# Zero fills moved from the FFN to the last stages and the end of a decode kernel, and six of eight outer products given to VectorE

## The chip, the cores and the metric

The kernel runs on one core of a Trainium2 chip. The metric is the device time of one execution, in microseconds (us). "Span" is the profiled execution from its first to its last instruction; it is 1.7 to 2.4 us shorter than the time of the same execution.

## The reference, cut to what matters

The kernel computes the output and all gradients of one decode step: conditioning (six vectors sa, ca, ga, sb, cb, gb from `silu(c) @ w_mod`), attention of one query over the last 4,096 of 65,536 cached keys and values, then a gated FFN.

```python
mod = (_silu(c) @ w_mod).reshape(c.shape[0], 6, 1, -1)
h = _layernorm(x) * (1 + ca) + sa
x = x + ga * A(h, k_cache, v_cache, wq, wo)     # attends to the last W = 4096 positions
h = _layernorm(x) * (1 + cb) + sb
x = x + gb * B(h, w_gate, w_up, w_down)         # h = sigmoid(g) * u; h @ w_down
# outputs: x, and the gradients of A_x, k_cache, v_cache, wq, wo, w_gate, w_up, w_down, c, w_mod
```

Positions that the window doesn't reach have gradient zero. So 61,440 of 65,536 rows of both cache gradients, 120 MiB in all, are only zeros that must be written. That is nearly half of the 256 MB which the kernel moves.

## The kernel before

The zeros are written by 120 transfers of 1 MiB ("fills"), issued from GpSimd between the real loads and stores. Lists at the head of the kernel say how many fills stand at each point of the program; `zero` takes the next ones and stops when none is left.

```python
Z_FFN = [3, 0, 3, 1, 4, 0, 3, 1, 4, 0, 3, 0, 3, 0, 4, 2, 3, 2, 3, 1, 3, 6, 0, 3, 1, 7, 3, 1]
...
def zero(n, after=None):
    for _ in range(n):
        if not zleft:
            return
        ins = nc.gpsimd.dma_start(out=zleft.pop(0).bitcast(FP32), in_=zeros[:, :])
        ...
```

The FFN goes through 14 blocks. Each loads 0.5 MiB of w_down and 1 MiB of w_up and w_gate, and turns the loaded tiles in place into their gradients, which it stores. A tile is loaded again when its store has landed. The last store of a block, the gradient of w_gate (`dwg_view`), is called the dWgate store below.

```python
for n in range(NB):
    ...                                            # front: matmuls with h; dug broadcast to all rows
    nc.sync.dma_start(out=wd_dram(out_8, n), in_=wd)
    ...                                            # per 128 rows: a reduction (VectorE), an outer product (ScalarE)
    nc.gpsimd.dma_start(out=dwu_view[:, :, n * FB:(n + 1) * FB], in_=ug[:, 0, :, :])
    st = nc.gpsimd.dma_start(out=dwg_view[:, :, n * FB:(n + 1) * FB], in_=ug[:, 1, :, :])
    if n + 2 < NB:
        dep(load_wd(n + 2), st)                    # the w_down load waits for the dWgate store
    zero(Z_FFN[2 * n])
    if n + 3 < NB:
        load_ug(n + 3)
    zero(Z_FFN[2 * n + 1])
```

The last stores are the sa/ca part of the gradient of w_mod: eight outer products of 128x2048 and eight stores of 512 KB.

```python
for j in range(KD):
    if j % 2 == 0:
        outer_act(s2_t[j], cs_col[:, j:j + 1], dmod_b2)      # ScalarE
    else:
        outer_dve(s2_t[j], cs_col[:, j:j + 1], dmod_b2)      # VectorE
    nc.gpsimd.dma_start(out=dwm_view[:, j, 0:2048], in_=s2_t[j])
    zero(0 if j < KD - 1 else len(zleft))
```

## Time and profile before

| | |
|---|---|
| Time | 632.7 us (632.57 to 632.85, 3 runs) |
| Span of the profiled run | 631.5 us (its time: 633.23) |
| Busy share: TensorE, VectorE, ScalarE, GpSimd | 29%, 51%, 34%, 22% |
| Moved | 70.3 MB read, 185.6 MB written |
| FFN, about 178 to 432 us | 404 GB/s |
| Later stages, 432 to 592 us | 422 to 424 GB/s |
| Tail, 592 to 626 us | 386, then 309 GB/s |

The costliest groups of the page have line, engine, operation, tiles and count; then busy time and the mean ns of one; then the engine's idle time before them and what ended it:

```profile
L139 POOL DMA_DIRECT2D out_dram<-zeros x120 | 65.1, 547 | 209.1 <-DMA out_dram<-zeros 51.3
L174 DVE CUSTOM_DVE_ANT_0 junk<-arena,b1k 128x1024 fp8e4<-128x1024 bf16 x28 | 34.3, 1224 | 111.3 <-DMA arena<-in_B_w_down_dram 110.8
```

The first line is the 120 fills: GpSimd often waits for an earlier transfer before it may issue the next (51.3 us for fills). In the trace its transfers take eight semaphores in turn, so no more than eight are in flight. The second line is the FFN's first work on a w_down tile: VectorE stands idle 110.8 us for those loads. That is not yet a loss. The loads stand in a full queue.

### The profile page before, as it was taken

How to read it: one execution, taken by the hardware profiler on the slowest of the kernel's cores; microseconds unless marked ns; L12 is line 12 of the kernel's file. 1: busy time of each engine (PE TensorE's matmuls, PEld its weight loads, DVE VectorE, ACT ScalarE, POOL GpSimd, SP SyncE). 2: the span in 40 equal slices, each digit the busy share in tenths (PEclk: the TensorE clock that was granted, in tenths of full speed). 3: DMA queues.
4: the chain of work that ended last, by engine and by line, in shares of the span. 5: the costliest groups of instructions: out<-in, count | busy, mean ns of one | idle time of the engine just before them, and what ended most of it. 6: DMA issues, size and time to landing. Idle time of an engine off the chain costs nothing.

```text
span 631.5 us, 8419 instructions
## 1 busy us (share of the span) xinstructions
PE 183.6 (29%) x3324; PEld 161.7 (26%) x3324; DVE 322.9 (51%) x726; ACT 215.4 (34%) x335; POOL 139.5 (22%) x224
## 2 busy tenths in 40 slices
PE   3977275532031110101111101102420950052440
PEld 3977154522021111101111101101310640042330
DVE  3532055204984552535555334507899760699421
ACT  2741165100044231333333023303686340042561
POOL 1001011113315132333332233222221111122021
PEclk9956598655555555555555555555555755555555
DMA  9999999999999999999999999999999999999986
GB/s 358 422 420 421 420 420 418 425 425 426 420 377 404 400 409 406 400 406 391 395 405 419 400 400 407 421 416 427 415 424 425 423 423 427 420 427 423 398 332 246
DMA packets 42183, 256.42 MB, mean 406 GB/s; under 512 B 4768, under 2 KB 4768, under 8 KB 17568
## 3 DMA queue, kind: packets, MB, share of 16 engines
q0 software_dynamic: 31104, 192.95, 80.4%
q1 hardware_dynamic: 10992, 62.93, 28.6%
q8 instruction: 26, 0.43, 0.3%
q14 instruction: 13, 0.11, 0.0%
q10 hardware_dynamic: 48, 0.01, 0.0%
HBM read 70.26 MB, written 185.60 MB: 405 GB/s over the span
## 4 chain that ended last, share of the span: by engine, by line
DMA 64%; DVE 17%; PE 7%; issue 5%; ACT 3%; POOL 2%; ACTq 0%; SPq 0%; DVEq 0%; POOLq 0%
DMA out_dram<-arena 25%; DMA arena<-in_B_w_down_dram 11%; DVE arena L174 7%; DMA arena<-in_A_wq_dram 7%; DMA arena<-in_A_v_cache_dram 6%; DMA arena<-in_B_w_gate_dram 5%; DMA arena<-in_A_wo_dram 4%; ACT arena L205 3%; DMA out_dram<-zeros 3%; DMA arena<-in_w_mod_dram 2%; DVE junk L174 2%; DVE arena L170 2%; DVE arena L178 1%; DVE fold_ps L178 1%; PE tp_kv L404 1%
## 5 line engine op out<-in xcount | busy, mean ns | idle before, releaser
L139 POOL DMA_DIRECT2D out_dram<-zeros x120 | 65.1, 547 | 209.1 <-DMA out_dram<-zeros 51.3
L174 DVE CUSTOM_DVE_ANT_0 junk<-arena,b1k 128x1024 fp8e4<-128x1024 bf16 x28 | 34.3, 1224 | 111.3 <-DMA arena<-in_B_w_down_dram 110.8
L600 PE MATMUL bc_ps<-ident_bf,dug_bf 128*128 128x128 bf16 x56 | 14.5, 475 | 214.4 <-DVE hh L157 214.4
L205 ACT ACTIVATE arena<-dug_b,h 128x512 bf16<-128x512 bf16 x112 | 71.4, 712 | 15.5 <-DVE dh2acc L174 15.5
L174 DVE CUSTOM_DVE_ANT_0 arena<-arena,dug_b 128x512 bf16<-128x512 bf16 x112 | 69.6, 684 | 0.0
L600 PEld LDWEIGHTS <-dug_bf 128*128 128x128 bf16 x56 | 7.8, 171 | 215.5 <-DVE hh L157 215.5
L602 ACT CAST dug_b<-bc_ps 128x512 bf16<-128x512 f32 x14 | 8.2, 586 | 159.4 <-PE bc_ps L600 159.4
L174 DVE CUSTOM_DVE_ANT_0 arena<-arena 128x1024 bf16<-128x1024 bf16 (+1 forms) x16 | 45.1, 2819 | 28.3 <-DMA arena<-in_w_mod_dram 26.2
L784 PEld LDWEIGHTS <-arena 8*128 8x128 bf16 x256 | 25.8, 131 | 76.7 <-issue 73.1
L174 DVE CUSTOM_DVE_ANT_0 arena<-arena,b1k 128x1024 bf16<-128x1024 bf16 x32 | 37.2, 1218 | 0.0
L502 POOL DMA_DIRECT2D arena<-in_B_w_up_dram x14 | 12.7, 909 | 90.3 <-DMA out_dram<-arena 77.7
L205 ACT ACTIVATE arena<-b1k,o_sh 128x1024 bf16<-128x1024 bf16 x24 | 27.2, 1152 | 11.0 <-DVE do_sh L174 11.0
L788 ACT CAST arena<-ps_kv 128x512 bf16<-128x512 f32 x32 | 16.1, 692 | 41.6 <-DMA out_dram<-arena 41.6
L166 DVE COPY arena<-tp_kv 128x1024 bf16<-128x1024 bf16 x19 | 13.0, 691 | 30.2 <-PE tp_kv L404 20.8
L404 PE MATMUL tp_kv<-ident_bf,arena 128*128 128x128 bf16 x256 | 21.2, 246 | 23.7 <-DMA arena<-in_A_k_cache_dram 13.8
L784 PE MATMUL ps_kv<-DO_hd,arena 8*128 8x128 bf16 x128 | 15.9, 296 | 41.6 <-ACT arena L788 41.6
L790 ACT ACTIVATE arena<-ps_kv 128x512 bf16<-128x512 f32 x32 | 16.1, 625 | 29.0 <-DMA out_dram<-arena 29.0
L313 PEld LDWEIGHTS <-arena 128*128 128x128 bf16 x320 | 25.3, 122 | 0.0
L404 PEld LDWEIGHTS <-arena 128*128 128x128 bf16 x256 | 18.4, 112 | 26.5 <-DMA arena<-in_A_k_cache_dram 14.7
L618 POOL DMA_DIRECT2D out_dram<-arena x14 | 12.6, 902 | 56.1 <-ACT arena L205 51.0
L784 PE MATMUL ps_kv<-Q_hd,arena 8*128 8x128 bf16 x128 | 16.1, 295 | 29.1 <-ACT arena L790 29.1
L407 ACT COPY arena<-tp_kv 128x1024 bf16<-128x1024 bf16 x13 | 13.2, 1012 | 33.0 <-PE tp_kv L404 33.0
(224 smaller groups left out, 481.0 us busy)
## 6 DMA issues: line engine op xcount, KB each, us to landing
out_dram<-zeros POOLq DMA_DIRECT2D x120, 1024.0 KB, 17.9
out_dram<-arena POOLq DMA_DIRECT2D x32, 1024.0 KB, 19.5
out_dram<-arena POOLq DMA_DIRECT2D x36, 512.0 KB, 11.5
arena<-in_A_wq_dram SPq DMA_DIRECT2D x16, 1024.0 KB, 15.3
arena<-in_w_mod_dram SPq DMA_DIRECT2D x8, 1536.0 KB, 19.2
arena<-in_A_wo_dram SPq DMA_DIRECT2D x8, 1024.0 KB, 40.7
arena<-in_B_w_down_dram SPq DMA_DIRECT2D x14, 512.0 KB, 10.9
arena<-in_B_w_up_dram POOLq DMA_DIRECT2D x14, 512.0 KB, 11.2
```

Of the source, the lines that this page charges most:

```text
L139: ins = nc.gpsimd.dma_start(out=zleft.pop(0).bitcast(FP32), in_=zeros[:, :])
L166: return nc.vector.tensor_copy(out=out, in_=a)
L174: return nc.vector.tensor_tensor_reduce(out=out, in0=w, in1=b, scale=1.0, scalar=0.0, op0=ALU.mult, op1=ALU.add, accum_out=acc)
L205: return nc.scalar.activation(out=out, in_=b, func=ACT.Copy, scale=col)
L313: nc.tensor.transpose(tp[:, nb * P:(nb + 1) * P], wm_t[j][:, c0:c0 + P], ident_bf[:, :])
L404: nc.tensor.transpose(tp[:, t8 * P:(t8 + 1) * P], src[:, g, t_ * DH:(t_ + 1) * DH], ident_bf[:, :])
L407: last = nc.scalar.copy(out=o, in_=tp[:, :])
L502: nc.gpsimd.dma_start(out=ug_slot[n % 3][:, 0, :, :], in_=wu_view[:, :, n * FB:(n + 1) * FB])
L600: nc.tensor.matmul(ps4[:, k // 2, :, k % 2], lhsT=r["dug_bf"][:, k:k + 1].broadcast_to([P, P]), rhs=ident_bf[:, :], start=(k == 0), stop=( ...
L784: nc.tensor.matmul(ps[:, t4 * DH:(t4 + 1) * DH], lhsT=rows[32 * g:32 * g + HG, t_ * P:(t_ + 1) * P], rhs=hd[32 * g:32 * g + HG, :], start= ...
L788: nc.scalar.copy(out=o, in_=ps[:, :])
L790: nc.scalar.activation(out=o, in_=ps[:, :], func=ACT.Copy, scale=float(scale))
```

## The change

The FFN gets 14 fills less: on average one per block. Four of them run in the last stages instead. Ten fills are held back and placed around the eight last stores, where the DMA share falls. And VectorE makes six of the eight sa/ca tiles, so that ScalarE's slower ones don't hold up the stores.

```diff
-Z_FFN = [3, 0, 3, 1, 4, 0, 3, 1, 4, 0, 3, 0, 3, 0, 4, 2, 3, 2, 3, 1, 3, 6, 0, 3, 1, 7, 3, 1]
+Z_FFN = [3, 0, 2, 1, 3, 0, 2, 1, 3, 0, 2, 0, 3, 0, 3, 1, 2, 2, 2, 1, 2, 4, 0, 3, 1, 5, 3, 1]
+Z_END = [4, 0, 0, 0, 2, 0, 0, 0, 4]
...
+    keep = [sum(Z_END)]
...
-            if not zleft:
+            if len(zleft) <= keep[0]:
                 return
...
+    keep[0] = 0
+    zero(Z_END[0])
     for j in range(KD):
-        if j % 2 == 0:
+        if j % 4 == 1:
             outer_act(s2_t[j], cs_col[:, j:j + 1], dmod_b2)
         else:
             outer_dve(s2_t[j], cs_col[:, j:j + 1], dmod_b2)
         nc.gpsimd.dma_start(out=dwm_view[:, j, 0:2048], in_=s2_t[j])
-        zero(0 if j < KD - 1 else len(zleft))
+        zero(Z_END[1 + j] if j < KD - 1 else len(zleft))
```

## The prediction

> **What bounds the kernel now.** I read the page's slices first, then the windows by stage, then the tail in windows of 1 us, the chain of waits, and at last the landing records of the single transfers in the trace. The slices:
>
> ```profile
> DMA  9999999999999999999999999999999999999986
> HBM read 70.26 MB, written 185.60 MB: 405 GB/s over the span
> ```
>
> The DMA engines have work in every slice but the last two, and no compute engine is above 51% of the span (VectorE). So the kernel is bound by moving 256.4 MB. The windows by stage (start:end, length, then busy time of PE, PEld, DVE, ACT, POOL, then clock, mean DMA share, GB/s) tell where it moves more slowly:
>
> ```profile
> 178.00:432.00 254.00, 32.14 (x712) 30.75 (x712) 122.40 (x377) 75.24 (x147) 76.59 (x110) 0.50 1.14 404
> 432.00:516.00 84.00, 35.97 (x567) 27.92 (x568) 73.15 (x148) 53.84 (x74) 16.22 (x29) 0.54 1.12 422
> 545.00:592.00 47.00, 15.28 (x124) 12.39 (x124) 46.45 (x39) 15.96 (x32) 10.46 (x17) 0.50 1.08 424
> 592.00:612.00 20.00, 11.51 (x142) 9.62 (x139) 1.59 (x11) 11.42 (x22) 3.69 (x7) 0.50 0.95 386
> 612.00:626.00 14.00, 0.37 (x1) 0.08 (x1) 4.11 (x13) 6.48 (x4) 4.72 (x8) 0.50 0.80 309
> ```
>
> The FFN (178 to 432) runs at 404 GB/s, the stages after it at 422 to 424, and the tail from 592 falls to 386 and 309. That fall is what the change aims at. In windows of 1 us:
>
> ```profile
> 611.00:612.00 1.00, 0.38 (x1) 0.08 (x1) 0.50 (x4) 1.00 (x1) 0.00 (x0) 0.50 0.54 221
> 612.00:613.00 1.00, 0.00 (x0) 0.00 (x0) 1.00 (x3) 1.00 (x2) 0.00 (x0) 0.50 0.13 51
> 613.00:614.00 1.00, 0.00 (x0) 0.00 (x0) 1.00 (x2) 1.00 (x1) 0.91 (x1) 0.50 0.06 25
> 614.00:615.00 1.00, 0.00 (x0) 0.00 (x0) 0.00 (x1) 1.00 (x2) 0.66 (x3) 0.50 0.37 152
> ...
> 626.00:627.00 1.00, 0.00 (x0) 0.00 (x0) 0.00 (x0) 0.00 (x0) 0.00 (x0) 0.50 0.07 29
> 627.00:628.00 1.00, 0.00 (x0) 0.00 (x0) 0.00 (x0) 0.00 (x0) 0.00 (x0) 0.50 0.07 29
> ```
>
> This looks like a hole of about 2.9 us (4 minus 0.54, 0.13, 0.06 and 0.37). But look at 613 and at 626 to 628: a share of 0.06 to 0.07, at 25 to 29 GB/s, is one engine of sixteen (1/16 is 0.0625) still at work. The mean hides one engine that is behind. The chain of waits has its mark:
>
> ```profile
> 601.05 14.98 DMA out_dram<-arena
> ...
> 616.06 0.75 DVE arena L170
> ```
>
> The last dWq store is issued at 601.05 and counts as landed only at 616.03, though the mean traffic had run out by 612. The trace records sixteen landings for each transfer, and they explain it. For that store fifteen are in by 609.83 and the sixteenth comes at 616.03; for the last dV/dK store 613.44 and 618.55. The sixteenth landings of the eight sa/ca stores are at 619.83, 621.08, 622.31, 623.57, 624.83, 626.07, 627.30 and 628.53: one per 1.24 us, 2.48 us per MiB, through the hole and to the end. From 545.80 to 628.53 that engine lands 33 MiB in 82.7 us, 2.51 us per MiB, with no gap. It has fallen behind since about 200 us (0.4 us there, 1 at 240, 3 at 400, 6 from 500 on). So the bound is one late DMA engine which never idles in the tail; the hole is in the other fifteen. Its losses are earlier: summing its landings against 2.475 us per MiB (the usual step of a zero fill), it is about 8 us behind at 200, 20 at 400, 25 at 542 and still 24 at the end. 244 MiB by 2.475 is 604 us; the 24 and 3 us after the last landing give the 631.5 us span.
>
> **What the Trainium skill says.** "Perfetto Trace Analysis", section What "DMA-bound" means, lists "Specific DMA engines" as one form of that bound; the trace agrees (one share of 0.06 alone at work). "DMA: Bandwidth & Descriptors", section Why a DMA increments its semaphore by 16 and not by 1: the engines finish independently and only the full sixteen means landed; the landings above show it, 6.2 us apart. The same page, Latency and other measured facts, says that DMA engines 7 and 15 are usually slower in traces; the trace shows one late engine but not its number. "VectorE: DVE Perf Modes", The perf-mode tier table, has 693 ns for a tensor_scalar of 2048 bf16; here 738 ns by the view below.
>
> **The change part by part.** The lists of fills hold more than the 120 regions, and `zero` stops when none is left, so I count what really runs. Before: 36 fills ahead of the FFN, 64 in it, 11 in the dWo stage, 9 in the last stages (the list there would allow 28), none at the end. After: 36, 50, 11, then 13 until ten are left, and 10 at the end (4 ahead of the first sa/ca store, 2 after the fourth, 4 after the last). Nothing is added or removed in bytes.
>
> - FFN: 14 fewer fills by 2.475 us = 34.7 us shorter, if the FFN stays bound by the transfers. Its own extra does not go with them. On the late engine, block periods of 6, 8 and 6 MiB took 16.01 (244.38 to 260.39), 20.55 and 16.65 us, so 1.2, 0.8 and 1.8 us over 2.475 per MiB: it belongs to the gate and up strips, not to the fills.
> - Last stages: 4 more fills, +9.9 us. VectorE is busy 46.5 of 47 us between 545 and 592, but GpSimd waits for free queue places there, so these fills lengthen the queue, not VectorE's work.
> - End: 10 fills, +24.75 us on the late engine. It had no gap, so none of it is hidden.
> - The sa/ca tiles:
>
> ```profile
> L205 ACT ACTIVATE arena<-arena,cs_col 128x2048 bf16<-128x2048 bf16 x4 | 7.7, 1990 | 0.0
> L170 DVE TENSOR_SCALAR arena<-arena,cs_col 128x2048 bf16<-128x2048 bf16 x4 | 2.8, 738 | 2.1 <-DMA out_dram<-arena 2.1
> ```
>
> ScalarE's share goes from 4 by 1.99 = 8 us to 2 tiles, 4 us; VectorE's from 4 to 6 by 0.74 = 4.4 us. The tiles can be ready about 3 us sooner, but four fills (10 us) now stand before them in the queue. Worth nothing on the path.
>
> Sum: -34.7 + 9.9 + 24.75 = 0. Bytes moved along a queue whose slowest engine is always full leave the time as it is: 632.7 us, give or take what the FFN's new pace and the fuller tail do to the engines' skew.
>
> **The rivals.**
> 1. The hole is real time. Then filling 611 to 615 (2.9 us) and the dip at 592 to 596 (share 0.85 of 4 us, 0.6 us) gives about 629. For it: the mean share, and ScalarE running 7.7 us without a pause ahead of the stores. Against it: the sixteenth landings, 1.24 us apart through the hole.
> 2. The FFN starves with fewer fills. Its loop runs through store landing and w_down load:
>
> ```profile
> 260.09 10.88 DMA out_dram<-arena
> ...
> 271.40 13.53 DMA arena<-in_B_w_down_dram
> ```
>
> Two blocks took 36.6 us from store to store (223.51 to 260.09), of which 23.9 are transfer waits (10.94 and 12.96) and about 12.7 compute. At 50 fills a block averages 3 + 3.57 = 6.57 MiB, 16.3 us and its extra 1.2, so 17.5; two are 35.0, and the waits must shrink to 22.3. Blocks of 16 us did run in a row (w_down loads issued at 289.80, 305.74, 321.73), and much of each wait is queueing, which falls as the queue empties. Should the blocks miss the full cut by 0.5 us each, the time is 632.7 + 7 = 640; if no block got shorter, 667, which I exclude.
> 3. The shorter queue after the FFN leaves a gap at the w_mod load that stalls VectorE (527.45 to 542.3, when nothing new is queued). When stores resume at 545.2, the late engine still has transfers to land until 558, 13 us of stock. I estimate the stock at the end of the FFN at some 5 us less (two fills fewer in the last blocks), so no gap; if there is one, +1 to 3 us.
> 4. The ends of the engines draw together in the tail. It helps only if the late engine gets faster when the others keep busy; nothing shows that.
>
> **Range and chances.** The null sum has 632.7. Rival 1, at about one in six, pulls down by up to 3.5 us; rivals 2 and 3, at about one in six, pull up by 2 to 7. I take 632.3, and 629.0 to 636.0 for 8 in 10. Two per cent is 12.7 us: more than the whole tail loss of rival 1, and reachable upwards only if the FFN clearly starves. So faster 0.02, same 0.95, slower 0.03.
>
> **What would show it.** Right: the mean DMA share stays full to the end with no hole near the sa/ca stores; the FFN ends some 30 to 35 us sooner; the sixteenth landings still run at 2.48 us per MiB to the end; the span moves by under 3 us although the hole is gone. Wrong: a gap in the sixteenth landings inside the FFN, or w_down waits that stay at 11 to 13 us with an FFN shortened by much less than 34 us (rival 2); or a span shorter by about the hole (rival 1), which would mean that the late engine was not the bound.

## The result, and the profile after

The changed kernel takes 634.44 us (634.29 to 634.70, 4 runs) against 632.78 us (4 runs): ratio 1.0027, 95% interval 1.0010 to 1.0044. A ratio is the mean time of one kernel's runs over that of the other's of the same rounds, so not quite the ratio of the medians quoted. The change is 0.3% slower; that is within the predicted range and within 2%.

The windows of the changed kernel, first by stage, then the place of the old hole:

```profile
178.00:400.00 222.00, 30.70 (x692) 29.39 (x692) 121.23 (x368) 74.74 (x146) 69.60 (x96) 0.50 1.11 395
592.00:612.00 20.00, 0.38 (x1) 0.08 (x1) 2.70 (x10) 0.00 (x0) 5.80 (x10) 0.50 1.10 423
...
612.00:613.00 1.00, 0.00 (x0) 0.00 (x0) 0.00 (x0) 0.00 (x0) 0.53 (x1) 0.50 1.04 418
613.00:614.00 1.00, 0.00 (x0) 0.00 (x0) 0.00 (x0) 0.00 (x0) 0.00 (x0) 0.50 1.13 442
...
625.00:626.00 1.00, 0.00 (x0) 0.00 (x0) 0.00 (x0) 0.00 (x0) 0.00 (x0) 0.50 0.07 25
```

The tail is repaired as intended: from 592 to 612 the core moves 423 GB/s instead of 386, and the hole is gone. Yet at 625 again one engine alone is at work (share 0.07), as before at 626 to 628. The last sixteenth landing is at 629.04 (628.53 before), the fifteenth of that transfer at 625.37 (626.61 before). Fifteen engines end 1.2 us sooner, the late one does not. The chain of waits, followed back from the last instruction (start us, length us, what), ends in the fills:

```profile
597.30 14.56 DMA out_dram<-zeros
611.87 0.28 issue
612.15 0.53 POOL out_dram L142
```

And the FFN has a new dip, at 395 GB/s against 404. These windows of 2 us show the place:

```profile
286.00:288.00 2.00, 0.00 (x0) 0.00 (x0) 0.42 (x2) 1.28 (x3) 0.00 (x0) 0.50 0.86 338
288.00:290.00 2.00, 0.00 (x0) 0.00 (x0) 1.78 (x3) 0.00 (x0) 1.94 (x3) 0.50 0.35 123
290.00:292.00 2.00, 0.30 (x2) 0.31 (x3) 1.56 (x8) 0.00 (x0) 1.46 (x3) 0.50 0.92 256
```

Before the change the middle one of them was

```profile
288.00:290.00 2.00, 1.53 (x29) 1.53 (x30) 0.84 (x6) 0.41 (x1) 0.91 (x1) 0.50 1.18 440
```

At 288 the mean share is now 0.35: all engines ran dry, the late one too. The stores issued at 288.06 and 288.94 landed at 292.18 and 294.19; they moved the sixteenth landing on by 1.75 and 2.01 us for 512 KB, where 1.24 is usual for the full queue of the tail. Such steps alone would not prove it: the kernel before has two of 1.75 and 2.00 late in its FFN (424.31, 452.77). The mark is that all sixteen landings of each of these two stores come within 0.6 us of each other, so all engines began on them together. In the FFN before they are never closer than 2.8 us for such a store, and no window of 2 us has a share under 0.94. It is the end of the sixth block, for which the new list has two fills only: 5 MiB in all.

The bookkeeping of the two profiled runs: the last dWgate store of the FFN lands at 418.52 instead of 452.77, 34.25 us sooner (14 fills are 34.65). From there to the last landing it takes 210.52 instead of 175.76 us, 34.76 more (14 fills again). So the last landing is 0.5 us later. The rest of the span's 1.17 us comes after it: GpSimd answers the closing barrier 2.19 us after SyncE's last drain, before it was 1.54 us.

### The profile page after: what moved, and what is told of

Its sections match the earlier page's. It is cut to its first block, busy times and chain, and to the rows that moved or that the text cites. A ratio compares the mean times of both kernels' runs of the same rounds, so it can differ in the third digit from the quotient of the medians.

```text
span 632.6 us, 8420 instructions
## 1 busy us (share of the span) xinstructions
PE 185.6 (29%) x3324; PEld 163.6 (26%) x3324; DVE 325.0 (51%) x728; ACT 211.6 (33%) x333; POOL 143.0 (23%) x224
## 4 chain that ended last, share of the span: by engine, by line
DMA 65%; DVE 12%; PE 8%; ACT 6%; issue 4%; POOL 2%; ACTq 0%; POOLq 0%; DVEq 0%; SPq 0%
DMA out_dram<-arena 29%; DMA arena<-in_B_w_down_dram 11%; DMA out_dram<-zeros 9%; DVE arena L177 6%; DMA arena<-in_A_v_cache_dram 6%; ACT arena L208 4%; DMA arena<-in_w_mod_dram 4%; DMA arena<-in_A_wo_dram 3%; DMA arena<-in_B_w_gate_dram 3%; DVE junk L177 2%; DVE arena L173 1%; PE tp_kv L407 1%; PE tm_w L316 1%; POOL out_dram L621 1%; PE bc_ps L603 1%
## 5 line engine op out<-in xcount | busy, mean ns | idle before, releaser
L177 DVE CUSTOM_DVE_ANT_0 junk<-arena,b1k 128x1024 fp8e4<-128x1024 bf16 x28 | 34.3, 1224 | 81.8 <-DMA arena<-in_B_w_down_dram 81.3
L603 PE MATMUL bc_ps<-ident_bf,dug_bf 128*128 128x128 bf16 x56 | 14.5, 475 | 185.9 <-DVE hh L160 185.9
L407 PE MATMUL tp_kv<-ident_bf,arena 128*128 128x128 bf16 x256 | 24.6, 270 | 21.7 <-DMA arena<-in_A_k_cache_dram 14.1
L407 PEld LDWEIGHTS <-arena 128*128 128x128 bf16 x256 | 21.5, 125 | 24.7 <-DMA arena<-in_A_k_cache_dram 15.0
L410 ACT COPY arena<-tp_kv 128x1024 bf16<-128x1024 bf16 x13 | 13.2, 1012 | 33.8 <-PE tp_kv L407 33.8
L316 PEld LDWEIGHTS <-arena 128*128 128x128 bf16 x320 | 24.3, 119 | 0.0
```

Of the source, the lines that this page charges most:

```text
L177: return nc.vector.tensor_tensor_reduce(out=out, in0=w, in1=b, scale=1.0, scalar=0.0, op0=ALU.mult, op1=ALU.add, accum_out=acc)
L316: nc.tensor.transpose(tp[:, nb * P:(nb + 1) * P], wm_t[j][:, c0:c0 + P], ident_bf[:, :])
L407: nc.tensor.transpose(tp[:, t8 * P:(t8 + 1) * P], src[:, g, t_ * DH:(t_ + 1) * DH], ident_bf[:, :])
L410: last = nc.scalar.copy(out=o, in_=tp[:, :])
L603: nc.tensor.matmul(ps4[:, k // 2, :, k % 2], lhsT=r["dug_bf"][:, k:k + 1].broadcast_to([P, P]), rhs=ident_bf[:, :], start=(k == 0), stop=( ...
```

## The experiments

New kernels could not use an fp8 output in the FFN's reduction, so all kernels below write that discarded output in bf16, and four small tiles that are never live in the FFN share its bytes. The two controls have this edit alone.

```diff
-    junk = vt([P, D], "junk", FP8)
+    junk = vt([P, D], "junk", BF16)       # moved up; rows24, DO_hd, do_col2, prod2, do_sh are slices of it
```

**Control before, c0.**

> Control: the kernel before, with the discarded output of two reductions in bf16 instead of fp8 (the check refuses the fp8 form in new kernels) and four small tiles moved into its bytes. All theories: within 0.15% of the kernel before (632.7, so 631.8 to 633.7), the reductions at 1.22 us as before.

Measured: 632.88 us (632.84 to 632.94, 5 runs), ratio to the kernel before 0.9997 (0.9984 to 1.0009); the reduction takes 1,224 ns as before.

**Control after, c1.**

> Control: the changed kernel with the same edit. All theories: 634.4, within 0.15% (633.5 to 635.4).

Measured: 635.17 us (634.75 to 635.56), ratio 1.0032 (1.0019 to 1.0046). The edit is harmless, and the loss of the change stands: 635.17 less 632.88 is 2.3 us here, 1.7 in the first pair. Its dry spot is there too. In c1 the last landing is 1.16 us later than in c0 and the end barrier 0.65 us longer; the other 0.5 of the 2.3 us lies outside the span (2.25 us of the time in the profiled run of c1, 1.78 in that of c0).

**Two fills in the hole, e1.**

```diff
+Z_END = [2, 0, 0, 0, 0, 0, 0, 0, 0]      # with the changed kernel's keep and zero(Z_END[0])
```

> The kernel before, with two of the nine fills of the last stages held back to the point just ahead of the first sa/ca store; FFN and the ScalarE/VectorE split untouched. Late-engine theory: the hole of the mean share near 611 to 615 us is gone (no 1 us window under 0.8 before the last 5 us), the late engine's landings keep 1.24 us per 512 KB, and the time stays within 1 us of its control (632 to 633.7). Hole theory: the time falls by 2.5 to 3.5 us, to 629 to 630.

Measured: 633.07 us (632.83 to 633.38), ratio 0.9999 (0.9987 to 1.0012). Windows of its tail:

```profile
612.00:613.00 1.00, 0.17 (x1) 0.08 (x1) 0.67 (x5) 1.00 (x1) 0.12 (x1) 0.50 1.04 422
613.00:614.00 1.00, 0.20 (x1) 0.00 (x0) 0.28 (x1) 0.19 (x1) 0.18 (x1) 0.50 1.03 418
...
622.00:623.00 1.00, 0.00 (x0) 0.00 (x0) 0.00 (x0) 0.00 (x0) 0.00 (x0) 0.50 0.09 37
626.00:627.00 1.00, 0.00 (x0) 0.00 (x0) 0.00 (x0) 0.00 (x0) 0.00 (x0) 0.50 0.07 29
```

The hole is filled, and the other engines are through by 623 instead of 626 (fifteenth landing of the last transfer: 622.93, 626.28 in c0), so the share falls under 0.8 sooner than in the last 5 us that I had written down. The late engine then works alone for five microseconds, and its last landing is at 628.15 (628.19 in c0). So the hole was idle time of engines that were ahead; filling it gives nothing. The rival that called it real time is refuted: it wanted 629 to 630.

**The split alone, e3.**

```diff
-        if j % 2 == 0:
-            outer_act(s2_t[j], cs_col[:, j:j + 1], dmod_b2)
-        else:
+        if j % 4 != 1:
             outer_dve(s2_t[j], cs_col[:, j:j + 1], dmod_b2)
+        else:
+            outer_act(s2_t[j], cs_col[:, j:j + 1], dmod_b2)
```

> The kernel before (control edit) with VectorE making six of the eight sa/ca tiles, fills untouched. Late-engine theory: the hole of the mean share gets shorter by 1 us or so and the time stays within 0.7 us of the control (632.2 to 633.6). If making the tiles sooner is worth something, or VectorE's extra tiles cost something, the time moves by 1 to 3 us.

Measured: 632.98 us (632.92 to 633.54), ratio 1.0002 (0.9989 to 1.0016); last landing 628.21. The split is worth nothing and costs nothing. That the hole would get shorter was wrong: between 611 and 615 it is 3.5 us long where c0 has 2.9, because GpSimd takes 1.82 us to issue the first store (1.03 in c0) and comes to the second at 614.47 instead of 613.77. In both runs that first issue ends 0.1 us after VectorE's run of tile products (614.35 in e3, 613.65 in c0), so it looks as if the added VectorE tiles held GpSimd up. The time does not follow the hole here either.

**The FFN list alone, e2.** Only the Z_FFN line of the change; nothing held back, the split as before.

> The kernel before (control edit) with the changed kernel's FFN list alone: 50 fills in the FFN, 23 after the dWo stage, none held back, the ScalarE/VectorE split as before. If the loss of the changed kernel comes from the FFN (its stock of queued transfers ran dry once, near 288 us), this kernel shows the same window of low share near 288 and the same loss: +1.3 to +2.5 us over the control, 634.2 to 635.5. If the loss comes from the ten fills at the end, it stays at 632 to 633.7.

Measured: 634.91 us (634.63 to 634.97), ratio 1.0029 (1.0017 to 1.0042), with the same dip:

```profile
288.00:290.00 2.00, 0.00 (x0) 0.00 (x0) 1.81 (x3) 0.00 (x0) 1.94 (x3) 0.50 0.39 137
```

The thinner FFN list makes nearly the whole loss (2.0 of the 2.3 us between the controls); the ten late fills and the split have little part in it.

**One fill given back, e7.**

```diff
-Z_FFN = [3, 0, 2, 1, 3, 0, 2, 1, 3, 0, 2, 0, ...
+Z_FFN = [3, 0, 2, 1, 3, 0, 2, 1, 3, 0, 3, 0, ...
```

> The changed kernel (control edit) with one fill given back to the sixth FFN block, the only one of the first ten or so that has two fills (51 in the FFN, 12 in the last stages). Theory of one dry spot: no window near 288 us with a mean share under 0.8, and the time falls by 1.0 to 2.0 us, to 633.2 to 634.2. If the loss is spread over all thinned blocks: falls by at most 0.3 us, 634.8 to 635.3.

Measured: 632.62 us (632.43 to 632.76), ratio to the kernel before 0.9994 (0.9982 to 1.0007). It is 2.5 us under c1, more than expected:

```profile
286.00:288.00 2.00, 0.00 (x0) 0.00 (x0) 0.58 (x2) 1.45 (x3) 0.00 (x0) 0.50 1.02 379
288.00:290.00 2.00, 0.00 (x0) 0.00 (x0) 0.00 (x0) 0.00 (x0) 1.76 (x2) 0.50 0.89 342
```

The period between two dWgate landings at this place is 14.37 us in c1 and 16.06 in e7. So the third fill of this block cost 1.69 us, where a fill costs 2.475 elsewhere: the fill that the change took away saved only that much, and had to be paid in full later. By the last dWgate landing (419.90 against 418.79) the fill that e7 has more has cost only 1.11 us, so 1.37 us (2.475 less 1.11) are won in the FFN: 0.79 in this block, the rest in others. That is nearly all of the 1.46 us by which the last landing comes sooner than in c1. And the end barrier is back at 1.54 us. The landing's 1.46 and the barrier's 0.65 make the span's 2.1 us.

**A second fill less per block, e6.** Z_FFN with 36 fills: one less again in each block, and 37 after the dWo stage.

> The kernel before (control edit) with one fill less again in each FFN block than in the changed kernel: 36 fills in the FFN, 37 after the dWo stage. Theory of the dry spots: a block then has 5 MiB or less and its transfers take some 13.6 us, less than the loop of store landing, w_down load and compute allows, so the share falls in most blocks and the time rises clearly: 637 to 645. If the stock is still enough nearly everywhere: 633 to 636.

Measured: 642.60 us (642.14 to 642.72, 4 runs), ratio 1.0150 (1.0133 to 1.0167). Its FFN:

```profile
178.00:378.00 200.00, 30.71 (x692) 29.40 (x692) 120.08 (x367) 74.80 (x146) 62.36 (x83) 0.50 1.07 374
```

The rate falls to 374 GB/s. The last dWgate store lands at 393.79, 58.6 us sooner than in c0, where 28 fills are 69.3: some 10.7 us are lost in the FFN, and 2.4 of them come back later. The last landing is 8.3 us later than in c0 and the end barrier takes 2.93 us. Blocks of 5 MiB have periods of 13.2 to 14.5 us against 12.4 for their bytes at 2.475 us per MiB. So the change stood at the edge of a slope, one dry block deep; c1 lost 1.06 us in the same reckoning (33.59 against 34.65).

**Sparing an engine, e4.** Three fills of 120 rows (the last region cut into 16 fills).

```diff
+                part = flat[0:n15].rearrange("(i p x) -> i p x", i=N15, p=120)      # N15 = 3
+                rest = flat[n15:].rearrange("(p x) -> p x", p=P)                    # 13 fills of 128 x 3840
```

> The kernel before, with three of the 1 MiB fills laid out over 120 rows instead of 128 (the last region cut into 16 fills, 121 in all), so that each of these three is spread over fifteen DMA engines. Late-engine theory: if the engine left out is the late one, it has three fills less, 3 x 2.32 us = 7 us less to do, the sixteenth landing lags by 6 us less at the end, and the time falls by 3 to 6 us, to 627 to 630. If another engine is left out, or the mean share is the bound, the time stays within 1 us (632 to 634) and the lag stays at 2 to 6 us.

Measured: 633.39 us (633.29 to 633.68), ratio 1.0005 (0.9993 to 1.0018). In the three fills one engine lands at once (478.16, 478.33, 478.50), but the sixteenth landing moves on by 2.3 to 2.55 us each time: the engine left out is not the late one. By itself that is inconclusive for the theory.

**Which engine, e5 and e8.** Seven fills of 64 KB per row and few rows; then nine fills of 100 to 126 rows.

```diff
+                for k in FEW:      # e5: [8, 12, 4, 14, 10, 6, 2] rows of 8 x 8 KB, contiguous in HBM
+                    few.append(flat[at:at + k * U].rearrange("(p c x) -> p c x", p=k, c=8))
```

> A measurement, not a candidate: the kernel before (control edit), with seven of the late fills cut to 8, 12, 4, 14, 10, 6 and 2 rows of 64 KB, so that a fill of k rows gives 64 KB to k DMA engines and nothing to the others. For each of them the sixteenth landing moves on by about 2.5 us if the late engine is among the k, and by under 0.5 us if it is left out. One late engine with a fixed number gives a single step: all fills of more rows than its number move it on, all of fewer rows don't. If there is no such order, the lag belongs to no fixed engine. Time: 2.5 us shorter for each fill that leaves the late engine out, until the others become the bound: 620 to 633.

> A measurement again: the kernel before (control edit), with nine of the late fills cut to 126, 117, 108, 110, 100, 119, 102, 124 and 122 rows, so that they should spread over 14, 13, 12, 11, 10, 7, 6, 4 and 2 DMA engines (the fills of 120 rows in the earlier run left the same engine out three times). For a fill that leaves the late engine out its sixteenth landing moves on by under 0.5 us, else by 2.4 to 3.1 us. If the fills take the first engines in order, there is one break: the late engine's number lies between the largest count that leaves it out and the smallest that takes it. If the pattern has no break, how fills of few engines are dealt out stays open.

Measured, one look each: 634.47 and 634.45 us. In e5 the sixteenth landing moves on by 2.56, 0.20, 2.39, 2.46, 0.19, 2.60 and 0.19 us: all or nothing, but not by the number of rows. What I had written down for a first-engines order fails. The steps fit a dealing in turn, each fill taking the next k of sixteen: then only the fifth or sixth engine of the turn is in the first, third, fourth and sixth fill and in no other. The Trainium skill has this ("DMA: Bandwidth & Descriptors", section Why a DMA increments its semaphore by 16 and not by 1: software-queue transfers on fewer than sixteen engines go to consecutive engines "from a round-robin cursor"). In e8 every fill moves the late engine: 2.52, 2.46, 2.20, 2.28 and 2.19 us for 126, 117, 108, 110 and 100 rows of 8 KB, which is 7 or 8 rows at 0.309 us. That agrees with the same section's exception (rows divided by 16 and rounded up, per engine) and not with my 14 to 10 engines. The late engine has its full rows in all of them, so it is not the last, short one.

The time expected for e5, 620 to 633 us, was missed: a fill of k rows spares some engines, but gives the ones that it uses more than an even split would. An estimate from 2.475 us per 64 KB: in e5 the late engine has four shares of 64 KB, 32 KB more than an even split of these fills, which is 1.2 us; the last landing is at 629.52, 1.33 us later than in c0. The same sum gives 0.8 us for e8 (measured 1.33) and 0.5 for e4 (measured 0.40). This was worked out afterwards, from one profile each, but the end follows the late engine's bytes in direction.

**A version that spares the late engine, e9, e10.** Both on top of e7.

```diff
+FEW = [12, 12, 12]                                         # e9: rows of 64 KB, the last three fills
+FEW = [(4, 4096), (2, 256), (10, 4096)] * 2                # e10: rows, elements per piece; eight pieces a row
+Z_END = [6, 0, 0, 0, 3, 0, 0, 0, 6]                        # e10
```

> The version with one fill back (e7), and the last three fills cut to 12 rows of 64 KB each, the form whose one fill left the late engine out in e5 (0.20 us instead of 2.5). Late-engine theory: the late engine has three shares of 0.75 MiB less, 3 x 1.86 = 5.6 us, the engines that are used have 3 x 0.62 = 1.9 us more; with a lag of 4.9 us in e7 both then end 3 us sooner, so the time is 628.5 to 631 against 632.6. If these fills are dealt out differently each time, or the late engine isn't the bound: 632 to 635.

Measured for e9: 632.23 us (631.97 to 632.88), ratio 0.9991 (0.9977 to 1.0005). The sixteenth landing moves on by 2.43, 2.45 and 0.19 us. So the dealing goes in turn, and the late engine was left out once, not three times. It saved 3 x 1.86 less 2 x 2.44, that is 0.7 us, and the last landing came at 627.20 instead of 627.89. That miss is in the expectation of the dealing; the gain in this profile is that of the late engine's work. The times of e9 and e7 overlap.

> The version with one fill back (e7), the end's fills still 10 MiB in all, but the last 1.77 MiB cut twice into fills of 4, 2 and 10 rows. In e5 and e9 the late engine's steps fit a dealing in turn, each fill of k rows taking the next k engines of sixteen: then the late one is number 4 or 5 of the turn, and here falls to the 2-row fill, which is only 8 KB. Late-engine theory: the late engine has 1.77 MiB less, 4.4 us, the others 2 x 0.3 = 0.6 us more; its last landing comes at about 623.6 instead of 627.9, level with the others, and the time is 628 to 630 against 632.6. If the dealing isn't in turn: the late engine's steps in these fills are 2.5 us somewhere and the time is 631.5 to 634. If the late engine isn't the bound: 632 to 634 although its landings draw level.

Measured for e10: 633.75 us (633.22 to 634.10), ratio 1.0009 (0.9995 to 1.0022): 1.1 us over e7. The late engine was spared: its first three small fills moved it on by 0.2 us each, to 625.04. But the end came at 628.96 all the same. With eight transfers in flight, each of the six small fills waited for an earlier one to land; the last was issued at 622.25. And four engines landed the second 4-row fill only at 628.3 to 628.6, some 8.7 us after its issue. Why so late is not settled. By what was written down, 632 to 634 us with level landings speaks against the late engine as the bound. But here other engines ended last, made late by the small fills themselves, so this trial shows neither that the late engine is no bound elsewhere nor a better kernel.

None of the versions beats the kernel before clearly: e7 (0.9994) and e9 (0.9991) have intervals that hold 1.

## Why the prediction was right or wrong

The prediction of 632.3 us, 629.0 to 636.0, holds the measured 634.44.

**The bound.** Right. The late engine's landings run at 1.24 us per 512 KB to the end in both kernels, and e1 settles it against the hole: filled, it moves the time by 0.2 us against the control (e3, with a longer hole, by 0.1). Nor did the engines draw together (rival 4): the last transfer's sixteenth landing is 3.67 us after its fifteenth, before 1.92. What makes that engine late was not found.

**The last stages and the end, 9.9 + 24.75 us.** Right: 34.76 us from the last dWgate landing to the last landing against 34.65. The fills in the tail are paid in full.

**The sa/ca tiles.** Right: worth nothing.

**The FFN, 34.7 us shorter.** This is the term that was mis-sized: the landing of the last dWgate store moved by 34.25 us in the first pair and 33.59 in the controls, so 0.4 to 1.1 us of the saving were not had. The step that failed is under rival 2: "At 50 fills a block averages 3 + 3.57 = 6.57 MiB". The average never runs dry. The thinnest block does, and the list shows it: two fills, 5 MiB, between blocks of 6. I also took blocks of 16 us in the trace as proof that the loop could follow; none of them was a 5 MiB block. c1's block of 5 MiB took 14.37 us.

**The gap that I looked for after the FFN (rival 3).** It did not come: no stage after the FFN lost landing time.

**What the prediction lacked.** 0.65 us of the loss lie after the last landing, in GpSimd's answer to the closing barrier: 1.54 us in c0, e1, e3 and e7, 2.19 in c1 and e2, 2.93 in e6, and 1.78 to 1.98 in e4, e5, e8, e9 and e10. Counted from the last landing to the end of GpSimd's last wait it is 2.78 us with the change's FFN list (c1, e2), 3.52 with 36 fills (e6) and 2.12 to 2.34 in all others, so most of it goes with the FFN list and not with the tail. Its cause stays open.

**The signs named.** The share is full at the old hole, the FFN's last landing is 34 us sooner (its last store is issued 28 us sooner, less than the 30 to 35 that I gave), the span moved by 1.2 us. The sign of rival 2, a gap in the sixteenth landings inside the FFN, was there too: a small true part of that rival, beside the null sum and not in its place. It put the measured time 1.7 us above the kernel before, where the prediction's centre had leaned 0.4 us below it.

## What to carry to other kernels

A dip in the mean DMA share is time to be won only if the slowest engine dips too: compare the sixteenth landing of each transfer with the fifteenth before moving work into it. Filler taken out of a stage pays only as long as every block keeps a full queue, so look at the thinnest block and not at the average. In a kernel that is bound by its transfers, as this one is, moving the same bytes to another place was worth nothing in itself; what could be won back was a dry spot.

## What the Trainium skill lacked or had wrong

- "DMA: Bandwidth & Descriptors", Bandwidth: one sentence says without a condition that for HBM and SBUF transfers the HBM limit of about 358 GB/s binds. This core alone moves 422 to 424 GB/s for long stretches (432 to 592 us). That agrees with the table of the same section, taken with one core at work; the sentence lacks that condition.
- The same page, Latency and other measured facts: engines 7 and 15 are named as usually slower. Here the late engine fits the fifth or sixth of the turn (e5, e9) and is not the last one (e8); the trace doesn't number it and where the turn begins isn't known, so engine 7 isn't excluded. And it is not slower in the tail, 2.48 us per MiB, but 2 to 6 us behind.
- "Perfetto Trace Analysis", What "DMA-bound" means: it names single engines as a bound and points to a track per engine, but has no way to see one in a trace that doesn't number the engines. Here the mean share showed a hole of 2.9 us whose filling was worth 633.07 against 632.88 us, nothing; the gap between the fifteenth and sixteenth landing showed it at once.
- No page says what lengthens GpSimd's answer to the closing barrier of the program, 1.54 us in c0 and 2.93 in e6 by the trace.
